# Attention heads' outputs transposed in 32x32 blocks on VectorE in place of TensorE, in a fused adaLN transformer block on one core

## The chip, the cores and the metric

The kernel runs on one core of one Trainium2 chip. The metric is device microseconds of one execution, taken as the median of several runs. Times inside the program come from one profiled execution of it.

## What is computed

One transformer block with adaptive layer norm, B = 1, S = 2048, D = 448, F = 1792, 16 heads of 28 columns, sliding window of 256, all in float32:

```python
mod = (silu(c) @ w_mod).reshape(1, 6, 1, D)       # sa, ca, ga, sb, cb, gb
h = layernorm(x) * (1 + ca) + sa
q, k, v = heads(h @ wqkv)                          # 16 heads of 28
p = softmax(where(0 <= i - j < 256, q k^T * 28 ** -0.5, -1e9))
x = x + ga * (merge_heads(p @ v) @ wo)
h = layernorm(x) * (1 + cb) + sb
x = x + gb * (mish(h @ w1 + b1) @ w2)
```

Every float32 product is made of several float32r passes: each operand is split into a high part (rounded to float32r) and a low part (the rest), and high*high, high*low and low*high are added.

## The kernel before

The rows are worked on in NG = 4 groups of 512 (`GT`). One group of attention is 16 heads, one head is 3 units (`BLOCKS`: six key blocks of 128 by the query blocks that see them), so there are 192 units, and one pass of the main loop (L930 to L981) issues one unit in a software pipeline. Names used below: g is the group, v the unit within it (0 to 47).

In pass u of that loop TensorE is given, in this order: `PV(u - 3, Pl)` (probabilities' low part times v, into the PSUM bank `pv`), `B(u)` (scores transposed, into `sB`, two banks, with mask and row maximum added by extra rows and a bf16 matmul), `A(a, t)` (scores of a head three ahead, into `sA`, two banks, read by VectorE for the row maximum), matmuls of a filler, and `PV(u - 2, Ph)`. ScalarE makes the two exponentials of the unit (`P`, `Ph`, L624 and L625), POOL (GpSimd) their difference `Pl` (L632). The filler (`fill_main`, L844) is a generator of the dense matmuls that belong to other places of the program: the qkv projection of this and the next group, `gen_oT` and `gen_wo` of the group before, `gen_hT` of the next. A second generator (`fill_side`, L863) has layer norm statistics, weights' loads and splits. A credit decides how much filler a unit gets: each pass adds `RATE[g]` (0.48, 0.91, 0.91, 0.65), each step of the filler takes off what it says it costs, and a step that gives no cost takes off `RATE[g]`. Every engine works through its instructions in the order written here; all DMAs stand in SP's queue.

What the change touches is the way from a head's result to the matmul with `wo`:

- `EV` (L646): ScalarE copies a head's result (60 rows: 28 of the high pass, the sum of the probabilities, 3 of zeros, 28 of the low pass; 512 columns) from the one `pv` bank into half of an SBUF tile `O2`. Two heads fill one tile.
- `E`, `E2`, `E3` (L649, L656, L660), once for two heads: four 128x124 transposes on TensorE into the PSUM bank `tr`, a ScalarE copy of the low part (L658), a VectorE reciprocal (L666) and addition (L667), and a POOL multiplication (L669) into `on`, which has rows on partitions and the 448 columns of all heads behind each other. At a group's last pair POOL also doubles the last 64 columns (L671).
- `gen_oT` (L506): when a group is complete, 16 transposes on TensorE (through `tr_chunk`, L232), four to a bank, turn `on` round; ScalarE makes the high part (L516), VectorE the low part (L511), reading the PSUM bank.
- `gen_wo` (L528): 11 passes of 448 columns to each of 4 row tiles, then the residual.
- `M2` (L586), once for two heads: a transpose of the row maxima into bank `tr`, split by VectorE into `mr`, sent by SP's queue into two rows of the `q` tiles. `B` of these heads waits for it.
- `gen_mod_wo` (L468): loads `wo` by rows of 128, scales it by ga on POOL, splits it (ScalarE high, POOL low).

## Time and profile before

| what | us |
|---|---|
| median of 3 runs (731.04 to 731.16) | 731.08 |
| span of the profiled execution, first to last instruction | 727.2 |
| the runs' median above that span | 3.9 |
| TensorE busy | 690.9 (95%) |
| ScalarE busy | 392.3 (54%) |
| VectorE busy | 381.4 (52%) |
| POOL busy | 331.2 (46%) |

In the profile PE is TensorE's matmuls, PEld its weight loads, DVE VectorE, ACT ScalarE and POOL GpSimd. A matmul's row has its own duration, longer than the step to the next matmul, because matmuls overlap; so a share of busy time says little of TensorE's slack, and prices on TensorE are read from the starts of neighbouring rows. Rows on ScalarE overlap by about a tenth of a microsecond in the same way. In the list of waits, "A <- B" is idle time of A that B's instruction ended. In a table by stage, each engine's busy time stands with its count of instructions. Attention runs from 56.4 us to about 422 us: group 0 to 133, group 1 to 235, group 2 to 337, group 3 to 422. Groups 1 and 2 go through the same steps 102 us apart.

### The profile page before, as it was taken

The numbers are of one execution on the slowest core, as the hardware profiler recorded it, in microseconds if no ns is written. First come the engines' busy times: TensorE is split into PE (matmuls) and PEld (weight loads), VectorE is DVE, ScalarE is ACT, GpSimd is POOL, SyncE is SP. The second block draws the span as 40 slices with busy tenths as digits, with TensorE's granted clock in tenths as the row PEclk, the third lists the DMA queues.
The fourth block names the chain that finished last, engine by engine and source line by source line (L and its number), as shares of the span: only waits on it lengthen the run. The fifth ranks groups of instructions, "written<-read, shape, count | busy, mean of one in ns | idle before, by whom it ended". The sixth has DMA issues, their size and how long they took to land.

```text
span 727.2 us, 11903 instructions
## 1 busy us (share of the span) xinstructions
PE 690.9 (95%) x3969; PEld 588.4 (81%) x3969; DVE 381.4 (52%) x1011; ACT 392.3 (54%) x740; POOL 331.2 (46%) x362
## 2 busy tenths in 40 slices
PE   3989989999999999999999899999999999999996
PEld 2767768888889888888887688888888888888885
DVE  4768645687765688655668942334333223322112
ACT  3516777676776667766878984344223222322221
POOL 4725697676666586766778955322010000000002
PEclk9898999999999999999999999999999999999999
DMA  8776564174483354471666175300300020001001
GB/s 201 213 239 190 186 200 135 56 234 130 123 260 132 115 173 147 137 217 56 182 202 191 48 239 166 115 13 1 102 0 1 1 101 1 1 1 51 1 0 51
DMA packets 48121, 83.86 MB, mean 115 GB/s; under 512 B 6126, under 2 KB 26108, under 8 KB 48060
## 3 DMA queue, kind: packets, MB, share of 16 engines
q1 hardware_dynamic: 48060, 83.10, 37.6%
q8 instruction: 32, 0.52, 0.3%
q14 instruction: 29, 0.24, 0.1%
HBM read 53.45 MB, written 29.36 MB: 114 GB/s over the span
## 4 chain that ended last, share of the span: by engine, by line
PE 69%; issue 11%; DVE 8%; ACT 5%; DMA 4%; POOL 2%; SPq 1%; POOLq 0%; DVEq 0%; ACTq 0%
PE z L820 15%; PE pv L642 8%; PE qk L294 7%; PE qk_v L294 5%; PE acc L1000 5%; PE acc L1001 5%; PE acc L999 5%; PE sA L580 4%; PE wo L294 4%; PE sB L610 4%; PE sB L621 3%; DVE junk L582 3%; ACT P L624 2%; PE et L653 1%; DMA wm<-in_w_mod_dram 1%
## 5 line engine op out<-in xcount | busy, mean ns | idle before, releaser
L632 POOL TENSOR_TENSOR Pl<-P,Ph 128x512 fp32r<-128x512 f32 (+2 forms) x192 | 232.9, 1221 | 80.9 <-ACT Ph L625 47.8
L582 DVE CUSTOM_DVE_ANT_0 junk<-sA,mask 128x384 f32<-128x384 f32 (+2 forms) x256 | 135.3, 529 | 100.7 <-PE sA L580 95.4
L828 DVE TENSOR_TENSOR al<-t,ah 128x512 fp32r<-128x512 f32 x56 | 38.8, 692 | 200.9 <-ACT ah L827 200.9
L624 ACT ACTIVATE P<-sB 128x512 f32<-128x512 f32 (+2 forms) x192 | 109.7, 571 | 63.0 <-PE sB L621 56.2
L826 ACT ACTIVATE t<-z,b1c 128x512 f32<-128x512 f32 x56 | 38.5, 688 | 188.6 <-PE z L820 177.7
L625 ACT ACTIVATE Ph<-sB 128x512 fp32r<-128x512 f32 (+2 forms) x192 | 109.3, 569 | 0.0
L580 PE MATMUL sA<-k,q 84*128 84x384 f32 (+2 forms) x256 | 101.0, 399 | 5.7 <-DVE mx L582 5.2
L820 PE MATMUL z<-hhf,w 128*128 128x512 f32 x224 | 89.5, 400 | 0.0
L820 PE MATMUL z<-hlf,w 128*128 128x512 f32 x224 | 88.8, 396 | 0.0
L999 PE MATMUL acc<-w2h,ah 128*128 128x448 f32 x224 | 82.1, 367 | 0.0
L1000 PE MATMUL acc<-w2l,ah 128*128 128x448 f32 x224 | 82.1, 367 | 0.0
L1001 PE MATMUL acc<-w2h,al 128*128 128x448 f32 x224 | 82.0, 366 | 0.0
L642 PE MATMUL pv<-Pl,v 128*60 128x256 f32 (+2 forms) x352 | 74.2, 285 | 5.1 <-POOL Pl L632 5.0
L642 PE MATMUL pv<-Ph,v 128*60 128x256 f32 (+2 forms) x352 | 76.9, 292 | 2.2 <-ACT o L647 2.0
L610 PE MATMUL sB<-q,k 86*128 86x256 f32 (+1 forms) x352 | 75.1, 287 | 0.4 <-DMA q<-mr 0.2
L820 PE MATMUL z<-hhf,w1l 128*128 128x512 f32 x168 | 66.3, 395 | 0.0
L610 PEld LDWEIGHTS sB<-q,k 86*128 86x128 f32 x352 | 62.2, 191 | 2.3 <-DMA q<-mr 0.6
L621 PE MATMUL sB<-fdmask,identr 128*128 128x128 bf16 (+1 forms) x320 | 60.5, 255 | 0.0
L580 PEld LDWEIGHTS sA<-k,q 84*128 84x128 f32 x256 | 49.3, 194 | 12.9 <-DVE mx L582 11.1
L642 PEld LDWEIGHTS pv<-Ph,v 128*60 128x60 f32 x352 | 45.5, 133 | 16.4 <-ACT o L647 4.3
L642 PEld LDWEIGHTS pv<-Pl,v 128*60 128x60 f32 x352 | 44.9, 132 | 16.2 <-POOL Pl L632 9.6
L1008 POOL TENSOR_TENSOR yo<-yo,x 128x448 f32<-128x448 f32 (+1 forms) x4 | 4.2, 1060 | 108.6 <-DVE yo L1005 108.6
(150 smaller groups left out, 1290.6 us busy)
## 6 DMA issues: line engine op xcount, KB each, us to landing
scr<-st SPq DMA_DIRECT2D x24, 512.0 KB
k<-scr SPq DMA_DIRECT2D x48, 252.0 KB
q<-scr SPq DMA_DIRECT2D x64, 168.0 KB
scr<-st SPq DMA_DIRECT2D x32, 256.0 KB
x<-x1d SPq DMA_DIRECT2D x10, 448.0 KB
xin<-in_A_x_dram SPq DMA_DIRECT2D x8, 448.0 KB
xr<-in_A_x_dram SPq DMA_DIRECT2D x16, 224.0 KB
x1d<-xr SPq DMA_DIRECT2D x16, 224.0 KB
```

The lines of the kernel that those rows point to most:

```text
L294: PE.matmul(p, b, a, start=(n == 0), stop=(n == 10))
L580: PE.matmul(p[:, c0:384], q[0:84, t * 128:(t + 1) * 128], k[0:84, t * 128 + c0:t * 128 + 384], start=True, stop=True)
L582: DVE.tensor_tensor_reduce(out=junk[:, c0:384], in0=p[:, c0:384], in1=mask[:, c0:384], scale=1.0, scalar=-3.0e38, op0=ALU.add, op1=ALU.max ...
L610: PE.matmul(p[:, c:c + 128 * (t1 - t0)], k[:, jj * 128:(jj + 1) * 128], q[:, t0 * 128:t1 * 128], start=(n == 0), stop=False, skip_group_ch ...
L624: ACT.activation(P[:, c0:], p[:, c0:], AF.Exp, scale=SCALE)
L625: ACT.activation(Ph[u][:, c0:], p[:, c0:], AF.Exp, scale=SCALE)
L632: eng.tensor_tensor(Pl[u][:, a:b], Pt[u][:, a:b], Ph[u][:, a:b].bitcast(F32), op=ALU.subtract)
L642: PE.matmul(pv[0:60, t0 * 128:t1 * 128], V[j % NV][:, h, :], P[u][:, c:c + 128 * (t1 - t0)], start=(P is Ph and b == 0 and n == 0), stop=F ...
L820: PE.matmul(zb[n], ps[m][1], ps[m][0], start=(m == 0), stop=(m == 10))
L999: PE.matmul(p, ah[n][:, ts], w2h[f], start=(f == 0), stop=False)
L1000: PE.matmul(p, ah[n][:, ts], w2l[f], start=False, stop=False)
L1001: PE.matmul(p, al[n][:, ts], w2h[f], start=False, stop=(f == NF - 1))
```

## The change

The four transposes per pair and the sixteen per group leave TensorE. `wo` is laid out anew so that each head has 32 rows (28 of `wo` and 4 of zeros). With that, a 32x32 block of four heads' results, stacked by 32 partitions, is in the right place for the matmul when every block is transposed by itself, which VectorE has an instruction for. It goes there and back: `EV` stacks four heads (high part and sum in `H4`, low part in `L4`), `N1` adds the two on POOL, `N2` turns the blocks (VectorE) and takes the reciprocal of the sums, `N3` multiplies on POOL, `N4` turns the blocks back into `on`, which is now already transposed. The four steps stand in passes u = 15, 16, 17 and 18, and every 12 passes after. `gen_oT` has no TensorE work left, and its VectorE subtraction reads two SBUF tiles. The bank `tr` is gone; `pv` has two banks, and `M2` takes its bank from `sA`. The padded `wo` is made in device memory by two DMAs early in the program. `wo` has a fourth low part, so `gen_wo` has 12 passes where it had 11.

```diff
+    wod = dram.tile([H, 32, D], F32, name="wod")
...
-    first = [(m, bank(tag, b, f"qk0_{m}"), qk_passes(0, m)) for m, tag, b in ((0, "pv", 1), (3, "tr", 1), (4, "sA", 2))]
+    first = [(m, bank(tag, b, f"qk0_{m}"), qk_passes(0, m)) for m, tag, b in ((0, "pv", 2), (3, "pv", 2), (4, "sA", 2))]
...
-    O2 = []
-    for i in range(2):
-        t = att.tile([128, GT], F32, name=f"o2_{i}")
-        POOL.memset(t[32:64, :], 0.0)
-        O2.append(t)
+    H4 = [att.tile([128, GT], F32, name=f"h4_{i}") for i in range(2)]
+    L4 = att.tile([128, GT], F32, name="l4")
+    POOL.memset(L4, 0.0)
...
-            split_lo(w, wo3[ci], wol[min(ci, 2)], ci, POOL)
+            POOL.tensor_tensor(wol[ci], w, wo3[ci].bitcast(F32), op=ALU.subtract)
...
-        def oT_out(p, ci):
-            DVE.tensor_tensor(ol[:, ci], p, oh[:, ci].bitcast(F32), op=ALU.subtract)
+        def oT_out(ci):
+            DVE.tensor_tensor(ol[:, ci], o[:, ci], oh[:, ci].bitcast(F32), op=ALU.subtract)
         for ci in range(4):
-            p = bank(tag, bufs, f"ot{g}{ci}")
-            tr_chunk([o[:, t] for t in range(4)], ci, p)
-            ACT.activation(oh[:, ci], p, AF.Copy)
-            pipe.add(1, lambda p=p, ci=ci: oT_out(p, ci))
+            ACT.activation(oh[:, ci], o[:, ci], AF.Copy)
+            pipe.add(1, lambda ci=ci: oT_out(ci))
...
-            for ci in range(3):
+            for ci in range(4):
                 ps += [(oh[:, ci, ts], wo3[ci]), (oh[:, ci, ts], wol[ci]), (ol[:, ci, ts], wo3[ci])]
-            ps += [(oh[:, 3, ts], wo3[3]), (ol[:, 3, ts], wo3[3])]
...
     def M2(pr):
-        p = bank("tr", 1, f"mt{pr}")
+        p = bank("sA", 2, f"mt{pr}")
...
-            pvb[i] = bank("pv", 1, f"pv{i}")
+            pvb[i] = bank("pv", 2, f"pv{i}")
...
     def EV(i):
-        r = 64 * (i % 2)
-        ACT.activation(O2[i // 2 % 2][r:r + 60], pvb[i][0:60, :], AF.Copy)
+        r, b = 32 * (i % 4), i // 4 % 2
+        ACT.activation(H4[b][r:r + 32], pvb[i][0:32, :], AF.Copy)
+        ACT.activation(L4[r:r + DH], pvb[i][32:60, :], AF.Copy)
...
+    def N1(qd):
+        POOL.tensor_tensor(H4[qd % 2], H4[qd % 2], L4, op=ALU.add)
+
+    def N2(qd):
+        oq[qd] = att.tile([128, 16, 32], F32, name=f"oq{qd}", tag="oq")
+        DVE.transpose(oq[qd].rearrange("p b j -> p (b j)"), H4[qd % 2])
+        rc4[qd] = att.tile([128, 16, 1], F32, name=f"rc{qd}", tag="rc")
+        DVE.reciprocal(rc4[qd], oq[qd][:, :, DH:DH + 1])
+
+    def N3(qd):
+        o = oq[qd][:, :, 0:DH]
+        POOL.tensor_tensor(o, o, rc4[qd].to_broadcast([128, 16, DH]), op=ALU.mult)
+
+    def N4(qd):
...
+        DVE.transpose(on[g][:, ci], oq[qd].rearrange("p b j -> p (b j)"))
...
+    later.append(lambda: dma(wod[:, 0:DH].rearrange("h r n -> h (r n)"), wo.rearrange("(h r) n -> h (r n)", r=DH)))
+    later.append(lambda: dma(wod[:, DH:32], L4[0:H, 0:D].unsqueeze(1).to_broadcast([H, 4, D])))
...
+        for w, f in ((15, N1), (16, N2), (17, N3), (18, N4)):
+            if u >= w and (u - w) % 12 == 0 and (u - w) // 12 < NS // 4:
+                f((u - w) // 12)
```

Beside that, E, E2 and E3 go, staging tiles shrink from 512 to 448 columns, and the buffers that hold `wo` (later w2) grow from 7 to 8.

How the order of instructions moves is seen at three places, all in the first units of group 1, where the results of group 0 are turned round. TensorE there, before: `ot` is a bank with four transposes of `on`, `sA` the scores for the row maximum, `pv` the head's result.

```order
L621 MATMUL sB_2001<-fdmask,identr 128x256
L580 MATMUL sA_1_2011<-k_3_359,q_1_351 128x384
L232 MATMUL ot_2021<-ident,on_911 128x128 x4
L580 MATMUL sA_2_2029<-k_3_359,q_1_351 128x384
L642 MATMUL pv_1966<-Ph_1944,v_144 60x128
```

TensorE at the same place, now:

```order
L618 MATMUL sB_1971<-fdmask,identr 128x256
L577 MATMUL sA_1_1981<-k_3_360,q_1_352 128x384
L577 MATMUL sA_2_1987<-k_3_360,q_1_352 128x384
L639 MATMUL pv_1931<-Ph_1913,v_145 60x128
L639 MATMUL pv_1931<-Ph_1913,v_143 60x384
```

The transposes are gone and nothing is put in their place: four units that had them have the attention's own matmuls alone. Between v = 4 and v = 11 the filler gave TensorE 11 dense matmuls before and gives 15 now; the units from 12 to 19 have 36 where they had 37. VectorE there, before (`hlo` is the low part of the turned result, `ot` lies in PSUM, `mx` the row maxima):

```order
L666 RECIPROCAL rc_2014<-et_1952 128x8
L667 TENSOR_TENSOR ol_1988<-ol_1988,et_1952 128x224
L582 ISA junk,mx_1885<-sA_2_2029,mask 128x384
L582 ISA mx_1885 128x1
L511 TENSOR_TENSOR hlo_2020<-ot_2021,hho_2019 128x512
L582 ISA junk,mx_1885<-sA_3_2049,mask 128x384
```

VectorE, now (`oq` and `on` are SBUF tiles):

```order
L579 ISA junk,mx_1848<-sA_0_1948,mask 128x384
L579 ISA mx_1848 128x1
L664 STREAM_TRANSPOSE on_1044<-oq_1890 128x512
L193 BN_STATS sta_1957<-xin_844 128x6
L194 BN_AGGR mva_1826<-sta_1957 128x2
L319 TENSOR_TENSOR st_6_1925<-qk_6_1860,st_6_1925 128x512
L511 TENSOR_TENSOR hlo_1955<-on_1044,hho_1954 128x512
L579 ISA junk,mx_1848<-sA_1_1981,mask 128x384
```

The reciprocal and the addition leave this place, a block transpose comes, and the subtraction no longer follows a TensorE instruction. POOL there, before (`Pl` is one unit's difference of exponentials):

```order
L207 TENSOR_TENSOR rsa_1993<-rsa_1993,mhalf 128x4
L632 TENSOR_TENSOR Pl_2009<-P_1977,Ph_1978 128x512
L669 TENSOR_TENSOR on_911<-ol_1988,rc_2014 128x4x56
L671 COPY on_911<-on_911 128x4x64
L632 TENSOR_TENSOR Pl_2047<-P_2005,Ph_2006 128x512
L632 TENSOR_TENSOR Pl_2073<-P_2043,Ph_2044 128x512
```

POOL, now (`h` is `H4`, `l` is `L4`):

```order
L648 TENSOR_TENSOR h_1_367<-h_1_367,l_368 128x512
L629 TENSOR_TENSOR Pl_1881<-P_1842,Ph_1843 128x512
L629 TENSOR_TENSOR Pl_1916<-P_1877,Ph_1878 128x512
L658 TENSOR_TENSOR oq_1890<-oq_1890,rc_1892 128x16x28
L629 TENSOR_TENSOR Pl_1946<-P_1912,Ph_1913 128x512
L208 TENSOR_TENSOR rsa_1960<-rsa_1960,mhalf 128x4
L629 TENSOR_TENSOR Pl_1979<-P_1942,Ph_1943 128x512
L629 TENSOR_TENSOR Pl_2006<-P_1975,Ph_1976 128x512
```

The multiplication and the doubling that stood among the `Pl` right behind `rsa` are gone from there; the multiplication of four heads stands two units earlier. In SP's queue the two DMAs for the padded `wo` stand behind the loads of the fifth head's q and k, ahead of the first later store of q and k.

64 lines of the change are left out of this document (21 added, 43 removed).

## Prediction

> **What bounds the kernel now.** I read the busy shares first, to see whether any engine is full:
>
> ```profile
> PE 690.9 (95%) x3969; PEld 588.4 (81%) x3969; DVE 381.4 (52%) x1011; ACT 392.3 (54%) x740; POOL 331.2 (46%) x362
> ```
>
> TensorE is, on average; the three others stand at half. But two thirds of the change lie in attention, which has stages of its own, so the next view is the busy time by stretch (length, then PE, PEld, DVE, ACT, POOL, the granted TensorE clock, the DMA engines' share and GB/s). The cuts follow the stages of the filler.
>
> ```profile
> 0.00:56.40 56.40, 40.14 (x170) 31.41 (x170) 36.38 (x85) 19.82 (x33) 25.76 (x63) 0.93 0.74 212
> 56.40:88.00 31.60, 29.98 (x186) 23.95 (x187) 24.82 (x78) 24.41 (x54) 19.99 (x21) 0.91 0.58 184
> 88.00:116.00 28.00, 25.03 (x167) 19.47 (x165) 13.98 (x57) 20.88 (x47) 25.95 (x28) 1.00 0.64 202
> 116.00:144.00 28.00, 27.82 (x182) 23.38 (x181) 17.08 (x61) 20.36 (x45) 19.06 (x20) 1.00 0.28 84
> 144.00:160.00 16.00, 15.21 (x111) 12.73 (x109) 13.16 (x40) 12.80 (x25) 12.47 (x14) 1.00 0.60 188
> 160.00:177.50 17.50, 17.30 (x116) 15.41 (x115) 13.77 (x39) 10.26 (x20) 11.23 (x13) 1.00 0.68 207
> 177.50:192.50 15.00, 14.13 (x107) 12.25 (x107) 13.73 (x39) 12.98 (x24) 11.27 (x11) 1.00 0.26 75
> 192.50:235.10 42.60, 42.60 (x289) 37.51 (x288) 24.39 (x82) 29.55 (x58) 27.28 (x23) 1.00 0.63 187
> 337.10:353.80 16.70, 16.62 (x108) 14.04 (x108) 8.75 (x30) 11.27 (x23) 10.81 (x10) 1.00 0.36 111
> 368.00:390.00 22.00, 22.00 (x157) 19.47 (x156) 14.97 (x49) 15.82 (x33) 16.32 (x15) 1.00 0.65 188
> 390.00:422.00 32.00, 27.85 (x208) 22.20 (x206) 28.65 (x70) 29.55 (x58) 30.60 (x30) 1.00 0.33 97
> 422.00:727.20 305.20, 298.42 (x1409) 257.68 (x1407) 90.68 (x145) 99.69 (x160) 40.54 (x49) 0.99 0.15 48
> ```
>
> TensorE fills the stretch, to 98% or more, in 116 to 144, 160 to 177.5, 192.5 to 235.1, 337 to 354, 368 to 390 and from 422 on; the stretches of group 1 have twins 102 us later in group 2. There a TensorE instruction less is time less. Elsewhere it has room: POOL bounds 88 to 116, and 390 to 422 has ScalarE, VectorE and POOL all near full. What TensorE waits for, in the list of waits (total us, times, longest):
>
> ```profile
> PE sA L580 <- DVE mx L582: 5.2, 13, 0.9
> PE pv L642 <- POOL Pl L632: 5.0, 12, 0.8
> PE pv L642 <- ACT o L647: 2.0, 2, 1.2
> ```
>
> **The change part by part.**
>
> *TensorE's transposes of heads.* What four of them cost is the difference of neighbouring starts (start, own duration, row):
>
> ```profile
> 220.21 0.59 PE L653 MATMUL et<-ident,o 124*128 124x124 f32 x4
> 220.55 0.45 PE L294 MATMUL qk_v<-wql,hh 128*128 128x448 f32 x1
> 220.84 0.36 PE L294 MATMUL qk_v<-wq,hl 128*128 128x448 f32 x1
> 221.05 0.37 PE L294 MATMUL qk_v<-wq,hh 128*128 128x448 f32 x1
> ```
>
> The four take 0.34 us (220.21 to 220.55), and the matmul behind them steps 0.29 where its like steps 0.21, so 0.43 in all. How many fall where TensorE is full, from the `et` rows of the same stretches alone (length, PE busy and count):
>
> ```profile
> 116.00:144.00 28.00, 1.17 (x8) 1.00 0.28 84
> 160.00:177.50 17.50, 0.59 (x4) 1.00 0.68 207
> 192.50:235.10 42.60, 2.35 (x16) 1.00 0.63 187
> 337.10:353.80 16.70, 0.59 (x4) 1.00 0.36 111
> 368.00:390.00 22.00, 1.17 (x8) 1.00 0.65 188
> 422.00:727.20 305.20, 0.59 (x4) 0.99 0.15 48
> ```
>
> With the twins of the second and third row that is 64 of 128, 16 groups of four: 16 x 0.43 = **-6.9 us**. The other 16 groups go from places that have room.
>
> *TensorE's transposes of `on`.* The same reading for a group's bank:
>
> ```profile
> 431.26 0.60 PE L232 MATMUL ot<-ident,on 128*128 128x128 f32 x4
> 431.61 0.48 PE L820 MATMUL z<-hhf,w 128*128 128x512 f32 x1
> 431.93 0.39 PE L820 MATMUL z<-hhf,w1l 128*128 128x512 f32 x1
> ```
>
> 0.35 to the next start, which steps 0.32 where 512 columns at the rate above (448 in 0.21) take 0.24: 0.43 again. Of 16 banks the four of group 3 lie here, behind 422: **-1.7**. The other twelve stand at the starts of groups, where TensorE has room.
>
> *The twelfth pass* of `wo` adds 16 matmuls of 448 columns at 0.21 (220.84 to 221.05). Four are behind 422, and I put three of the other twelve in full stretches, since the order has more dense work at v = 4 to 11 and less at 12 to 19: 7 x 0.21 = **+1.4**. Full stretches together: **-7.2**.
>
> *ScalarE, POOL and VectorE* pay for it. Groups of instructions (busy, mean ns | idle before):
>
> ```profile
> L647 ACT ACTIVATE o<-pv 60x512 f32<-60x512 f32 x64 | 37.8, 590 | 22.5 <-PE pv L642 21.6
> L658 ACT ACTIVATE ol<-et 128x224 f32<-128x224 f32 x32 | 11.7, 364 | 0.0
> L632 POOL TENSOR_TENSOR Pl<-P,Ph 128x512 fp32r<-128x512 f32 x155 | 200.0, 1294 | 72.9 <-ACT Ph L625 40.7 <-POOL Pl L632 9.5 <-PE pv L642 8.3
> L669 POOL TENSOR_TENSOR on<-ol,rc 128x224 f32<-128x224 f32 x32 | 18.9, 592 | 23.1 <-ACT Ph L625 11.0 <-DVE ol L667 10.5 <-PE sA L580 1.0
> ```
>
> ScalarE's rows overlap by 0.1, so a copy of 512 columns is 0.48 and one of 224 is 0.26. Per head one long copy is added and half a short one goes, +0.35; over 64 heads +22 us. POOL gets per four heads `N1` (shape and kind of `Pl`: 1.29) and `N3` (twice the columns of `on`: 1.1) for two `on`: +1.2, over 16 tiles +19. Where this binds:
>
> - 88 to 116: the `on` of three pairs leave and one and a half tiles come: 1.5 x 2.4 - 3 x 0.59 = 1.8 on an engine with 2.0 us of room that was already waited for. **+1.5**.
> - 390 to 422: about six heads' share, POOL +1.8, ScalarE +2.0, on engines with 1.4 and 2.5 us of room, and VectorE has 3.3. **+2.5**.
> - In the full stretches both engines have a quarter to a third of room; nothing, but TensorE's gain shrinks that cover by a fortieth.
>
> *VectorE.* No row of before shows the block transpose. The nearest rows by size are a read of 448 columns in SBUF, and the same engine's SBUF to SBUF operation, which spreads widely (min/median/max):
>
> ```profile
> L192 DVE BATCH_NORM_STATS2 stw<-xr 128x6 f32<-128x448 f32 x16 | 10.0, 628 | 0.5
> L222 DVE TENSOR_SCALAR xin<-xin,mva,rsa x12: 498/854/1499, 50.5 to 268.7; 128x448 f32<-128x448 f32 x12
> L667 DVE TENSOR_TENSOR ol<-ol,et 128x224 f32<-128x224 f32 x32 | 10.7, 335 | 0.0
> L666 DVE RECIPROCAL rc<-et 128x8 f32<-128x8 f32 x32 | 6.5, 203 | 0.0
> ```
>
> So 0.5 to 1.5 us; I take 0.65, by the first row, which holds its time. Then per tile 2 x 0.65 + 0.2 replaces 2 x (0.335 + 0.203): +0.4, 7 us in all, beside TensorE's work nearly everywhere, and TensorE no longer waits in line with it. At 1.5 it would be +34 us; that is the first rival. *A rule against the change:* the Trainium skill, VectorE: DVE Perf Modes, section "Rules for kernel authors", gives a 128x128 transpose to TensorE wherever PSUM will do as its destination, and its section "The three transpose paths" has VectorE at 311 ns for 128x128 in bf16. Four of those are an estimate of 1.24 us a tile of 512 columns; by it VectorE gets 19 us more than by 0.65, of which TensorE would feel perhaps an eighth, and the sum would end near 728. No row of before shows it, and both lie within the range.
>
> *The starts of groups 1 and 2* (144 to 160). POOL's multiplication and doubling left of `Pl`:
>
> ```profile
> 153.81 0.40 POOL L671 COPY on<-on 128x256 f32<-128x256 f32 x1
> 155.50 0.45 PE L642 MATMUL pv<-Pl,v 128*60 128x256 f32 x2 [0.41 <-POOL Pl L632]
> ```
>
> The `Pl` that TensorE waits for stands 0.96 us earlier (0.40 and an `on`); the next link, VectorE's row maximum, is close behind, and its `hlo` keeps its length. **-0.8** each, -1.6. At 177.5 to 192.5 and its twin a transpose group goes where TensorE has 0.9 room: -0.3 each, **-0.6**. At 56 to 88 two groups, 0.86, of which two thirds count: **-0.6**.
>
> *Banks.* The second `pv` bank ends waits for the copy of a result, 2.0 us at most in the list above; **-1.0**, as the copies themselves come later. `M2` now takes one of two `sA` banks. 13 of 256 users of these waited, 5.2 us, 0.02 apiece; 32 more users would add 0.65, and if each waited like those 13 (0.4), 12.8. I take **+0.8**, since the 243 others didn't wait.
>
> *The start.* The padded `wo` copies 0.8 MB in device memory, 1.6 MB read and written. At the 212 GB/s of the first stretch that is 7.6 us if everything behind it in SP's queue waits; the queue's next entries are stores and loads of q and k, whose first use lies several us behind. Between 0 and 7.6 I take **+0.7**: the DMA share is 0.74, so most fits in.
>
> Sum: -7.2 + 1.5 + 2.5 - 1.6 - 0.6 - 0.6 - 1.0 + 0.8 + 0.7 = -5.5. The profiled execution's span is 727.2, the median of the runs 731.08, 3.9 above; that part stays. **731.1 - 5.5 = 725.6 us.** Its own range is 721 to 729.5: the small terms at their favourable ends, or `M2`, the start and a long transpose at +4 together.
>
> **The rivals.**
>
> *Slower: VectorE becomes the late link.* The row of L222 above shows one kind of VectorE instruction at 0.50 and the same one at 1.50; the subtraction that reads PSUM does not stretch:
>
> ```profile
> L511 DVE TENSOR_TENSOR hlo<-ot,hho 128x512 fp32r<-128x512 f32 x16 | 11.0, 686 | 6.6 <-ACT hho L516 6.6
> ```
>
> If what stretches L222 is POOL at work in SBUF (a `Pl` is 1.29 us long), then 32 transposes and the twelve `hlo` within attention, which now read and write SBUF alone, may each take 0.43 longer (its mean of 0.93 less 0.50): 44 x 0.43 = 19 us, with the 7 above 26 us. They stand in line ahead of row maxima. VectorE is tight in 56 to 88, 144 to 160, 177.5 to 192.5, their twins and 390 to 422, some 126 of 366 us of attention, a third: +9, and **735** (732.5 to 738). It decides from 0.3 us apiece (5.5 over 44 instructions, of which the tight third counts in full and the rest in a tenth: 5.5 / 18 = 0.3). For it: the spread, and 5.2 us of waits for the row maximum already. Against: VectorE is half idle, and a single delay of 0.4 is mostly covered by `sA`'s second bank. The Trainium skill, SBUF — State Buffer, section "SBUF: two separate sides", has a lock behind such a spread: one port pair is held for a whole instruction by GpSimd, or by a VectorE operation in a 2-port mode or with two SBUF inputs. By it `hlo` would wait and a block transpose, with one source, need not, which halves this rival; the trace agrees so far as L222 and L511 go. Chance 0.27.
>
> *The full gain.* All TensorE work that goes counts: 48 x 0.43 - 16 x 0.21 = 17.3, and with the `pv` waits, less M2 and the start, **713**. Against it: POOL at 25.95 of 28.00 and 30.60 of 32.00 can't give way. Chance 0.10.
>
> *No change.* ScalarE's 22 us and POOL's 19 us more bind wherever TensorE gave room, so that the full stretches turn into ones bounded by the probabilities: **731**, within 1.4. For it: ScalarE's 29.55 and POOL's 27.28 of 42.60 hide a rhythm in which TensorE waits for each unit in turn. Chance 0.13. That the second bank of `pv` does nothing would cost the forecast 1 us only.
>
> **How the numbers follow.** The forecast has 0.50. Faster by more than 0.2% (1.5 us, about what a measurement of this kernel can tell from no change) are the forecast and the full gain: 0.60. Same 0.13, slower 0.27. For 8 in 10 the range leaves out the far end of the full gain and the far end of the slower case: 715 to 737.
>
> **What would show it.** Right: 192.5 to 235 and its twin get shorter by 1.5 us or more each, the end from the last unit to the last instruction by 1.5, and 88 to 116 and 390 to 422 get longer, with POOL near full. The block transpose has a mean of 0.6 to 0.8. Wrong: transposes or `hlo` of over 1 us, and row maxima as the first releaser of TensorE, with more than 10 us (first rival); a start of attention later than 58 us (the DMAs); waits of `M2`'s transposes or of `sA` above 8 us (the bank); or 88 to 116 no longer than before (full gain).

## The result, and the profile after

Median 736.14 us (733.82 to 737.49, 7 runs) against 731.08 (728.18 to 732.45, 7 runs): the ratio is 1.0069, interval 1.0046 to 1.0092. The change makes the kernel slower by 0.7%; forecast were 725.6 us and faster. The busy shares:

```profile
PE 684.7 (93%) x3793; PEld 578.0 (79%) x3793; DVE 398.8 (54%) x995; ACT 422.3 (58%) x772; POOL 351.5 (48%) x357
```

TensorE lost 176 instructions and 6 us of busy time, ScalarE got 30 us, POOL 20 and VectorE 17. To find the place, I cut the span of the changed kernel at its own units: the start, group 0, then for each group its units 0 to 3, 4 to 15 and the rest (group 3: 16 to 27 and 28 to 46), and what lies behind the start of the last unit. Columns as before.

```profile
0.00:58.27 58.27, 40.28 (x170) 31.79 (x171) 36.82 (x85) 20.52 (x34) 25.21 (x62) 0.94 0.79 228
58.27:134.84 76.57, 71.49 (x441) 55.59 (x441) 50.25 (x171) 64.26 (x139) 61.58 (x61) 0.96 0.54 164
134.84:145.64 10.80, 10.62 (x63) 8.67 (x63) 5.83 (x20) 7.94 (x16) 5.61 (x6) 1.00 0.24 77
145.64:172.58 26.94, 24.47 (x147) 20.78 (x146) 23.23 (x60) 19.97 (x37) 21.17 (x20) 0.87 0.62 188
172.58:236.29 63.71, 62.40 (x427) 54.73 (x426) 45.70 (x133) 51.81 (x96) 46.85 (x39) 1.00 0.56 167
236.29:247.25 10.96, 10.80 (x64) 8.84 (x64) 5.88 (x19) 7.88 (x15) 5.76 (x6) 1.00 0.14 41
247.25:274.57 27.32, 24.68 (x148) 20.59 (x146) 22.92 (x60) 19.97 (x37) 21.18 (x20) 0.88 0.59 185
274.57:338.29 63.72, 62.41 (x427) 54.75 (x426) 45.70 (x133) 51.81 (x96) 46.83 (x39) 1.00 0.51 152
338.29:347.19 8.90, 8.90 (x57) 7.53 (x57) 4.61 (x16) 7.06 (x14) 4.62 (x5) 1.00 0.17 52
347.19:371.44 24.25, 21.16 (x134) 17.32 (x133) 16.80 (x45) 20.56 (x39) 20.66 (x17) 0.93 0.63 199
371.44:393.04 21.60, 21.60 (x152) 19.07 (x150) 15.39 (x48) 17.88 (x34) 15.30 (x13) 1.00 0.68 198
393.04:426.86 33.82, 26.53 (x182) 20.28 (x181) 29.97 (x65) 30.23 (x58) 32.04 (x30) 0.97 0.25 73
426.86:732.97 306.11, 299.36 (x1403) 258.04 (x1402) 95.74 (x147) 102.45 (x164) 44.68 (x49) 0.99 0.16 49
```

The same cuts in the kernel before; shown are the stages that will matter, units 4 to 15 of groups 1 to 3 and the last units of group 3:

```profile
144.10:168.21 24.11, 23.32 (x166) 20.01 (x164) 19.89 (x55) 17.99 (x35) 18.05 (x21) 1.00 0.67 210
...
246.20:270.34 24.14, 23.39 (x165) 20.00 (x164) 19.93 (x55) 17.99 (x35) 18.00 (x21) 1.00 0.68 209
...
346.31:368.04 21.73, 21.45 (x158) 18.77 (x157) 14.06 (x46) 18.21 (x36) 16.25 (x15) 1.00 0.70 218
...
390.10:419.84 29.74, 25.59 (x193) 20.47 (x192) 27.59 (x66) 27.29 (x54) 28.52 (x29) 1.00 0.32 92
```

All stages, us:

| stage | before | after | difference |
|---|---|---|---|
| start, to the first scores | 56.45 | 58.27 | +1.8 |
| group 0 | 76.91 | 76.57 | -0.3 |
| units 0 to 3 of groups 1, 2, 3 | 10.74, 11.08, 9.22 | 10.80, 10.96, 8.90 | -0.4 |
| units 4 to 15 of groups 1, 2, 3 | 24.11, 24.14, 21.73 | 26.94, 27.32, 24.25 | +8.5 |
| units 16 to 47 of groups 1, 2 | 66.91, 66.75 | 63.71, 63.72 | -6.2 |
| units 16 to 27 of group 3 | 22.06 | 21.60 | -0.5 |
| units 28 to 46 of group 3 | 29.74 | 33.82 | +4.1 |
| behind | 307.35 | 306.11 | -1.2 |

The sum is +5.8, the difference of the spans of the two profiled executions (the medians differ by 5.1). So the gain was there and was given back at three places of 24 to 27 us each, and in group 3's last units. In units 4 to 15, where the last group's results are turned round, VectorE, ScalarE and POOL are all at least 73% busy in groups 1 and 2, and the granted clock stands below 1. TensorE's scores wait there for VectorE's row maxima, 2.1, 2.3 and 3.1 us in groups 1, 2 and 3; in the kernel before the list of the same units has no such wait. The whole span has 10.0 us of it (5.2 before):

```profile
PE sA L577 <- DVE mx L579: 10.0, 13, 1.5
```

VectorE's rows there, low part of the turned result (`hlo`), and the two block transposes:

```profile
L511 DVE TENSOR_TENSOR hlo<-on,hho 128x512 fp32r<-128x512 f32 x16 | 20.4, 1278 | 2.8 <-ACT hho L514 2.8
...
L652 DVE STREAM_TRANSPOSE oq<-h 128x512 f32<-128x512 f32 x16 | 11.4, 710 | 5.0 <-POOL h L648 4.8
L664 DVE STREAM_TRANSPOSE on<-oq 128x512 f32<-128x512 f32 x16 | 11.3, 708 | 3.7 <-POOL oq L658 3.7
```

The transposes take 0.71 us, near the 0.65 estimated. The subtraction took 0.686 when it read PSUM and takes 1.278 now, as a mean of values from 0.68 up. How the row maxima get late, from VectorE's rows and POOL's at the start of group 1 (start, duration):

```profile
150.77 0.71 DVE L664 STREAM_TRANSPOSE on<-oq 128x512 f32<-128x512 f32 x1
...
152.12 0.66 DVE L319 TENSOR_TENSOR st<-qk,st 128x512 fp32r<-128x512 f32 x1
152.70 0.68 DVE L511 TENSOR_TENSOR hlo<-on,hho 128x512 fp32r<-128x512 f32 x1
153.30 0.55 DVE L579 CUSTOM_DVE_ANT_0 junk<-sA,mask 128x384 f32<-128x384 f32 x1
153.77 0.08 DVE L579 DVE_READ_ACCUMULATOR2_ANT mx<- 128x1 f32 x1
...
156.60 1.79 DVE L511 TENSOR_TENSOR hlo<-on,hho 128x512 fp32r<-128x512 f32 x1 [0.68 <-ACT hho L514]
158.31 0.55 DVE L579 CUSTOM_DVE_ANT_0 junk<-sA,mask 128x384 f32<-128x384 f32 x1
```

```profile
153.62 7.31 POOL L629 TENSOR_TENSOR Pl<-P,Ph 128x512 fp32r<-128x512 f32 x5
```

POOL works without a gap on five `Pl`, and the subtraction that starts at 156.60 lasts 1.79 us: its own 0.69 and most of a `Pl`. The row maximum behind it (`junk`, `mx`) starts at 158.31 only. TensorE's scores wait for both maxima shown:

```profile
153.91 0.44 PE L577 MATMUL sA<-k,q 84*128 84x384 f32 x1 [1.31 <-DVE mx L579]
...
158.92 0.69 PE L577 MATMUL sA<-k,q 84*128 84x384 f32 x1 [0.75 <-DVE mx L579]
```

So there are two things. The first and longer wait stands behind a subtraction of 0.68 us, which nothing held up: between two row maxima VectorE has a block transpose, statistics, `st` and the subtraction in line, as the order ahead of the prediction showed. Only the second wait stands behind a stretched one. The four subtractions of this group take 0.68, 0.96, 1.79 and 1.76 us.

What happens to TensorE's clock meanwhile (the third column from the right):

```profile
152.00:154.00 2.00, 0.69 (x7) 0.42 (x5) 1.83 (x6) 1.98 (x5) 1.62 (x3) 1.00 1.00 351
154.00:156.00 2.00, 1.63 (x10) 1.24 (x11) 1.92 (x5) 1.96 (x5) 2.00 (x2) 0.84 1.04 267
156.00:158.00 2.00, 2.00 (x10) 1.60 (x9) 1.40 (x1) 2.00 (x5) 2.00 (x3) 0.50 0.85 226
158.00:160.00 2.00, 1.25 (x4) 1.04 (x4) 1.97 (x7) 1.15 (x3) 2.00 (x2) 0.50 0.13 43
160.00:162.00 2.00, 2.00 (x8) 1.66 (x8) 1.96 (x3) 0.00 (x0) 1.58 (x2) 0.50 0.10 15
```

Two microseconds in which TensorE is busy for 0.69, then, from 155.3 on, about 7 us at half speed. The second group has the same, group 3 half as much. Busy time of TensorE there is therefore no sign of more work.

### The profile page after: what moved, and what is told of

It reads as the page before. It is cut to its first block, busy times and chain, and to the rows that moved or that the text cites. A ratio compares the mean times of both kernels' runs of the same rounds, so it can differ in the third digit from the quotient of the medians.

```text
span 733.0 us, 11603 instructions
## 1 busy us (share of the span) xinstructions
PE 684.7 (93%) x3793; PEld 578.0 (79%) x3793; DVE 398.8 (54%) x995; ACT 422.3 (58%) x772; POOL 351.5 (48%) x357
## 4 chain that ended last, share of the span: by engine, by line
PE 70%; issue 12%; DVE 7%; ACT 4%; DMA 4%; POOL 3%; SPq 0%; POOLq 0%; DVEq 0%; ACTq 0%
PE z L814 15%; PE pv L639 9%; PE qk L296 7%; PE wo L296 6%; PE sA L577 5%; PE acc L993 5%; PE acc L994 5%; PE acc L992 5%; PE sB L607 4%; PE qk_v L296 4%; PE sB L618 3%; DVE junk L579 2%; DMA wm<-in_w_mod_dram 1%; PE qk L403 1%; ACT P L621 1%
## 5 line engine op out<-in xcount | busy, mean ns | idle before, releaser
L629 POOL TENSOR_TENSOR Pl<-P,Ph 128x512 fp32r<-128x512 f32 (+2 forms) x192 | 236.3, 1244 | 90.2 <-ACT Ph L622 46.3
L639 PE MATMUL pv<-Pl,v 128*60 128x256 f32 (+2 forms) x352 | 76.9, 293 | 10.3 <-POOL Pl L629 8.5
L607 PE MATMUL sB<-q,k 86*128 86x256 f32 (+1 forms) x352 | 77.2, 294 | 2.4 <-DMA q<-mr 1.8
L607 PEld LDWEIGHTS sB<-q,k 86*128 86x128 f32 x352 | 63.8, 197 | 4.8 <-issue 2.3
L639 PEld LDWEIGHTS pv<-Ph,v 128*60 128x60 f32 x352 | 47.6, 136 | 14.0 <-issue 1.2
```

Source lines behind the costliest of these rows:

```text
L607: PE.matmul(p[:, c:c + 128 * (t1 - t0)], k[:, jj * 128:(jj + 1) * 128], q[:, t0 * 128:t1 * 128], start=(n == 0), stop=False, skip_group_ch ...
L629: eng.tensor_tensor(Pl[u][:, a:b], Pt[u][:, a:b], Ph[u][:, a:b].bitcast(F32), op=ALU.subtract)
L639: PE.matmul(pv[0:60, t0 * 128:t1 * 128], V[j % NV][:, h, :], P[u][:, c:c + 128 * (t1 - t0)], start=(P is Ph and b == 0 and n == 0), stop=F ...
```

## The experiments

Three theories: (1) TensorE stands idle for want of other work, its clock falls, and that is the cost; (2) VectorE's subtraction, held up by POOL, is the late link; (3) the bank that the row maxima's transpose now shares. Since up to 134 us most of the kernels below run the same instructions and yet group 1 starts at 134 to 141 us in their profiles, I judge each by its stage as well as by its median. The stage is units 4 to 15 of a group (26.94, 27.32 and 24.25 us in the changed kernel); a table at the end of this section has it for all runs. Medians of different runs are compared through their ratios to the kernel before, which was measured again beside each (changed kernel: 1.0069).

**Dense work in the gap.**

```diff
+            p = bank("mm" if g < NG - 1 else "tr", 2, f"ot{g}{ci}")
+            for n in range(4):
+                PE.matmul(p[:, 0:D], wo3[n][:, 0:128], wo3[n], start=(n == 0), stop=(n == 3))
             ACT.activation(oh[:, ci], o[:, ci], AF.Copy)
```

> The changed kernel with four dense matmuls of 448 columns (result unused) added to each of the 16 steps that turn a group's result round, where TensorE had its transposes before. Theory 1 (clock): TensorE stands idle there, so its granted clock falls to 0.50 for 3.4 or 6.8 us in four places, about 10 us of half speed in sum; with dense work there the clock stays above 0.95 in 144 to 168 and its twin, and the time falls to 731 to 733 though TensorE does 13 us more work. Theory 2 (VectorE's subtraction, stretched by POOL from 0.69 to 1.28 us, is what holds TensorE, the clock is a by-product): the added work comes on top, 737 to 741, and VectorE stays the releaser. Theory 3 (the bank of M2): no less waiting for sA, 736 to 740.

740.77 us, ratio to before 1.0136 (1.0114 to 1.0159). The stage in group 1:

```profile
150.92:177.47 26.55, 24.83 (x164) 21.66 (x162) 23.68 (x60) 19.97 (x37) 21.25 (x20) 1.00 0.62 191
```

The clock holds at 1.00, and the stage takes 26.55 us in groups 1 and 2 and 22.72 in group 3: 0.4, 0.8 and 1.5 less than in the changed kernel, not the 2.5 to 3.2 that were lost. That is 2.7 of the 8.5 us, and not all of it can be the clock's: a run below without the padded copy (`direct_wo`) has the changed kernel's own instructions in this stage, and takes 26.51 us in group 1 with the clock at 1.00 and nothing added, and in group 3 22.70 us, as short as here, with the clock at 0.92. The median is higher through the start and group 0, which the edit doesn't touch and which differ between profiles, and through 3.2 us behind attention, where the added work of group 3 stands.

**TensorE's old transposes, unused.**

```diff
+            p = bank("mm" if g < NG - 1 else "tr", 2, f"ot{g}{ci}")
+            tr_chunk([o[:, t] for t in range(4)], ci, p)
             ACT.activation(oh[:, ci], o[:, ci], AF.Copy)
```

> The changed kernel with the old 16 transposes of four 128x128 blocks a group put back on TensorE, result unused (0.43 us each step, 7 us of TensorE work in all). Theory 1 (clock): TensorE is busy a little more in the places where the clock falls; if transposes count as activity the clock holds at some of them and the time is 732 to 735; if not, the clock falls as before and the time is 736 to 738. Theory 2 (VectorE): 736 to 738, the four of group 3 behind attention cost 1.7.

745.41 us, ratio 1.0211 (1.0187 to 1.0235), far beyond every forecast. The stage in group 1, and a wait of group 3's transposes behind attention:

```profile
148.97:175.76 26.79, 23.41 (x164) 20.45 (x162) 23.23 (x60) 19.97 (x37) 20.88 (x20) 1.00 0.60 189
```

```profile
PE ot L233 <- DVE on L666: 4.5, 1, 4.5
```

The loss is in that last place: the part behind attention is 315.8 us long, 9.7 more, since these transposes stand in TensorE's line ahead of the feed-forward matmuls and wait for VectorE's last block transpose; the wait shown is 4.5 of the 9.7. In attention the clock holds at 1.00 through the stage, and it still takes 26.8: the clock again isn't the bound. This run is the base for the one below that gives the subtraction an operand in PSUM.

**No subtraction.** `oT_out` is left out, and the low passes read the high part:

```diff
-            pipe.add(1, lambda ci=ci: oT_out(ci))
...
-                ps += [(oh[:, ci, ts], wo3[ci]), (oh[:, ci, ts], wol[ci]), (ol[:, ci, ts], wo3[ci])]
+                ps += [(oh[:, ci, ts], wo3[ci]), (oh[:, ci, ts], wol[ci]), (oh[:, ci, ts], wo3[ci])]
```

> The changed kernel without the 16 VectorE subtractions for the low part of the turned result; the matmuls that read it read the high part again, so the low part's product is wrong by that much. VectorE loses 20 us, 15 of them at the starts of groups 1 to 3. Theory 2 (the stretched subtraction): TensorE's longest wait for the row maximum (1.31 us at the start of group 1) goes, the time falls by 5 to 8, to 728 to 731, and the clock stays at 1. Theory 1 (idle TensorE since its filler has nothing to give): the units there are bounded by the probabilities and VectorE anyway, TensorE idles on, the clock still falls in one or two of the places, 732 to 735. Theory 3 (bank): under 2 us less, 734 to 736.

729.56 us, ratio 0.9990 (0.9970 to 1.0010): 0.8% less than the changed kernel, level with the kernel before. The stage in groups 1 and 3:

```profile
148.60:173.41 24.81, 23.09 (x147) 19.91 (x146) 18.54 (x56) 19.97 (x37) 20.07 (x20) 0.93 0.65 204
```

```profile
346.92:367.64 20.72, 19.54 (x134) 16.12 (x133) 12.43 (x41) 19.46 (x38) 16.89 (x14) 1.00 0.72 213
```

24.8 and 20.7 where the changed kernel has 26.9 and 24.3; group 2 gains less, 26.2 for 27.3. The time is as theory 2 forecast, but the clock still falls in groups 1 and 2, which theory 2 had not expected. And the run takes away the whole subtraction, which the kernel before has too and fits into 24.1 us.

**The banks as before** (`pv` one bank, the maxima's transpose one of its own):

```diff
...
-        p = bank("sA", 2, f"mt{pr}")
+        p = bank("mt", 1, f"mt{pr}")
...
-            pvb[i] = bank("pv", 2, f"pv{i}")
+            pvb[i] = bank("pv", 1, f"pv{i}")
```

> The changed kernel with the banks as they were before: one for the heads' results and one of its own for the transposed row maxima. Theory 3 (bank): waits of the row-maximum scores for VectorE fall from 10.0 to about 5 us, the time by 3 to 5, to 731 to 733, and the clock falls in fewer places. Theories 1 and 2: no change in the places where the clock falls, 735 to 738 with the waits for the copy of a result back (2 us).

740.78 us, ratio 1.0166 (1.0122 to 1.0209). Waits of the whole span:

```profile
PE pv L639 <- ACT l L645: 12.3, 23, 1.6
...
PE sA L577 <- DVE mx L579: 9.1, 12, 1.6
```

The scores wait for VectorE nearly as much as in the changed kernel (9.1 us for 10.0), and the time grows, so as an account of the whole loss theory 3 falls. What comes back is the wait for the copy of a result: 12.3 us where the kernel before had 2.0. The copy has become two, and the second `pv` bank hides that; the two bank edits together are worth 4.0 us by the profiled spans (737.0 for 733.0), not 0.2. By stage it is less simple: with the old banks group 0 takes 3.0 us more and units 16 to 47 of groups 1 and 2 take 2.0 more each, but units 4 to 15 take 1.4, 1.8 and 1.3 less. Theory 3 is therefore not ruled out for the stage itself.

**The subtraction with one operand in PSUM**, by way of TensorE's transposes, for the results of groups 0 to 2 (the blocks are turned once more, so the output differs):

```diff
+            s = o[:, ci]
+            if g < NG - 1:
+                s = bank("mm", 2, f"ot{g}{ci}")
+                tr_chunk([o[:, t] for t in range(4)], ci, s)
-            ACT.activation(oh[:, ci], o[:, ci], AF.Copy)
-            pipe.add(1, lambda ci=ci: oT_out(ci))
+            ACT.activation(oh[:, ci], s, AF.Copy)
+            pipe.add(1, lambda ci=ci, s=s: oT_out(ci, s))
```

> The changed kernel with the 16 TensorE transposes a group put back for groups 0 to 2, into a bank that ScalarE's high part and VectorE's low part now read in place of the SBUF tile (the blocks are turned a second time, so the result differs). VectorE's subtraction then reads one operand in PSUM. If two SBUF operands are what lets POOL hold it up, its mean falls from 1.28 to about 0.69 us in these groups (12 of 16), and against the run with transposes but the SBUF operand (units 4 to 11 of group 1 in 18.2 us, 18.2 in group 2) those units take 16 to 17 us; the time is 730 to 733. If the length of the subtraction is not what counts, but TensorE's lack of other work, those units stay at 18 us and the time at 735 to 738. The run with transposes had lost 9.7 us behind attention by group 3's; here these are left out, and the end behind the last unit is back at 306 us.

732.45 us, ratio 1.0029 (1.0015 to 1.0043). The subtraction's two forms, and the stage in group 1:

```profile
L511 DVE TENSOR_TENSOR hlo<-ot,hho 128x512 fp32r<-128x512 f32 x12 | 8.2, 686 | 5.0 <-ACT hho L518 5.0
...
L511 DVE TENSOR_TENSOR hlo<-on,hho 128x512 fp32r<-128x512 f32 x4 | 5.2, 1328 | 0.5 <-ACT hho L518 0.5
```

```profile
148.19:173.66 25.47, 23.48 (x163) 20.41 (x162) 20.82 (x60) 19.97 (x37) 19.77 (x20) 1.00 0.63 199
```

In one kernel, 0.686 us with an operand in PSUM (the results of groups 0 to 2) and 1.328 with both in SBUF (those of group 3, behind attention). At the same place, the stage of group 1, the run with the same transposes and the operand in SBUF has 0.68, 0.98, 1.35 and 1.78 us, and this run 0.68 to 0.69 four times. At the same clock of 1.00 the stage is shorter than in that run by 1.3, 1.1 and 1.0 us in groups 1, 2 and 3, and TensorE's waits for row maxima in the whole span fall from 10.7 to 4.8 us: the hold-up costs about 3.4 us. Theory 2 is shown, but it isn't the whole 8.5.

**ScalarE's second copy and POOL's addition left out**, singly and together. The low pass of the heads' results is then missing from the output.

```diff
-        ACT.activation(L4[r:r + DH], pvb[i][32:60, :], AF.Copy)
```

> The changed kernel without ScalarE's second copy of each head's result (64 copies of 28 rows, 0.5 us each; the low pass of the probabilities is left out of the result). Tells the cost of ScalarE's added work, 31 us. If ScalarE bounds the tail of group 3 (units 28 to 47, 33.8 us against 29.7 before) and the POOL-bound stretch hardly gains, the tail falls by 3 to 4 us and the time to 731 to 733; if POOL bounds it, the tail falls by under 1 us and the time is 734 to 736. The clock falls at the starts of groups as before.

```diff
-        POOL.tensor_tensor(H4[qd % 2], H4[qd % 2], L4, op=ALU.add)
+        pass
```

> The changed kernel without POOL's addition of the two halves (16 of 1.29 us, the low pass left out of the result). If POOL bounds the tail of group 3 and the units 20 to 35 of group 0 (units 28 to 31 took 8.60 us there, 6.56 before), these two places give back 2 and 1 to 2 us and the time is 732 to 733.5; if ScalarE bounds the tail, only the 1 to 2 us of group 0 come back, 734 to 735.5.

> The changed kernel without the second copy on ScalarE and without the addition on POOL (the low pass left out of the result). Each alone left the last 20 units of group 3 at 33.8 and 35.6 us (33.8 with both, 29.7 in the kernel before). If these units are bounded by ScalarE and POOL in turn, taking both away brings them to 30 to 32 us and the time to 726 to 729; if something else bounds them (VectorE, or a clock that falls), they stay above 33 and the time is 729 to 731.

729.79 us (ratio 0.9999, 0.9984 to 1.0015) without the copy, 738.29 (1.0112, 1.0079 to 1.0145) without the addition, 727.91 (0.9965, 0.9947 to 0.9983) without both. First the stage in group 1 without the copy, then the last units of group 3 without the addition, then these without both:

```profile
146.41:171.68 25.27, 22.20 (x148) 18.62 (x146) 22.65 (x60) 17.71 (x33) 21.05 (x22) 1.00 0.64 200
```

```profile
395.62:431.24 35.62, 28.05 (x182) 21.79 (x181) 32.10 (x65) 30.78 (x58) 28.79 (x28) 0.90 0.23 69
```

```profile
385.89:418.88 32.99, 26.06 (x183) 20.89 (x181) 31.00 (x65) 26.55 (x51) 28.69 (x27) 0.95 0.25 73
```

My expectation put the copy's price in the tail of group 3; it lies in the stage, 1.7, 2.0 and 2.6 us, and without both the stage is the same within 0.1 us. The tail stays at 33.9 without the copy, and 33.0 without both. In the kernel before POOL was 96% busy there (28.52 of 29.74); in the changed kernel it is 95% (32.04 of 33.82), with 3.5 us more busy time. But without both POOL is back at 28.69 and ScalarE below its old 27.29, and the tail still takes 3.3 us more than before; VectorE then stands at 94% (31.00 of 32.99). That VectorE holds the tail is only argued, since no run takes its work away there. Why POOL's addition left out makes the whole slower (738.3) I can't settle: of the 5.4 us that its profile is longer than the changed kernel's, 3.5 are at the start, ahead of the first instruction left out, and the clock is at 0.90 in the tail and 0.82 in group 2's stage.

**Useful dense work in the gap**: six of the output projection's matmuls that need the high part alone, two in each turning step but the first (the other two of the eight stand behind the last step, in `gen_wo`).

```diff
+            if g < NG - 1 and ci:
+                wo_mms(g, ci - 1)
...
+    def wo_mms(g, ci):
+        oh, ol = OT[g]
+        for n, b in enumerate((wo3, wol)):
+            PE.matmul(WO0[g][:, 0:D], oh[:, ci, 0:128], b[ci], start=(ci + n == 0), stop=False)
+        for cj in range(4 if ci == 3 else 0):
+            PE.matmul(WO0[g][:, 0:D], ol[:, cj, 0:128], wo3[cj], start=False, stop=(cj == 3))
...
```

> The changed kernel with the first eight dense matmuls of the output projection's first row tile (those that need the high part alone) issued between the four steps that turn a group's result round, two a step, and its low passes at the end. TensorE gets 0.4 us of useful work in each of the units where it stood idle, with no work added. Theory 1 (idle TensorE lets the clock fall): the clock falls in fewer of the four places, the time is 732 to 734. Theory 2 (VectorE's stretched subtraction is the bound): 735 to 737, the same waits for the row maximum.

735.68 us, ratio 1.0103 (1.0053 to 1.0154), no measurable change. The stage in group 1:

```profile
148.47:174.96 26.49, 23.16 (x152) 19.32 (x150) 23.37 (x60) 19.98 (x37) 20.35 (x19) 1.00 0.67 208
```

The clock stays at 1.00 in groups 1 to 3, and the stage takes 26.49, as long as with dense filling though no work is added: theory 2's forecast.

**The DMA for the padded `wo`**, and the kernel before again:

```diff
     def gen_mod_wo():
+        later.append(lambda: dma(wod[:, 0:DH].rearrange("h r n -> h (r n)"), wo.rearrange("(h r) n -> h (r n)", r=DH)))
...
-    later.append(lambda: dma(wod[:, 0:DH].rearrange("h r n -> h (r n)"), wo.rearrange("(h r) n -> h (r n)", r=DH)))
```

> The changed kernel with the large one of the two added DMAs (784 KB of wo into its padded place in device memory) issued not ahead of attention but in front of the loads that read it, behind the group's layer norm. If it is what keeps the row maxima's small DMA from landing (TensorE's first scores waited 1.80 us for it, none before), attention starts at 55.5 to 57.5 us instead of 58.3 (58.3 to 61.8 in the other runs that have it) and the time falls by 1.5 to 3.5, to 732.5 to 734.5. If the later start is chance, attention starts at 58 to 61 and the time stays at 735.5 to 737.

> The kernel before, profiled a second time, to see how much the start of attention and each group differ between two profiles of one program. Theory that the added DMAs delay the start: attention starts at 56.0 to 57.5 again. Theory that the start is chance: it lies anywhere from 56 to 62. Each group within 0.5 us of the first profile (76.9, 101.8, 102.0, 82.7).

738.04 us (1.0105, 1.0084 to 1.0126) and, one run, 728.89. The kernel before starts attention at 56.43 us in the second profile (56.45 in the first), group 0 takes 77.08, and the three stages repeat within 0.04 us. The changed kernel's first scores:

```profile
58.27 0.41 PE L607 MATMUL sB<-q,k 86*128 86x384 f32 x1 [1.80 <-DMA q<-mr]
```

They wait 1.80 us for the 4 KB transfer of the row maxima, which has 784 KB ahead of it. With the big transfer later, attention starts at 57.10 and the first scores wait 0.3, but the wait returns some units on (2.3 us of the 2.6):

```profile
PE sB L608 <- DMA q<-mr: 2.6, 2, 2.3
```

and group 0 takes 80.6 us, 4.0 more, of which this wait explains 2.3. Over all runs the link is plain: in the twelve profiles that issue the big transfer ahead of attention the first scores wait 1.7 to 4.0 us for row maxima, in the four that don't 0.3 to 0.6.

**The subtraction on POOL** (`DVE.tensor_tensor` to `POOL.tensor_tensor` in `oT_out`):

> The changed kernel with the subtraction for the low part moved from VectorE to POOL (16 of 1.29 us, both operands in SBUF). There is then no VectorE instruction there that POOL could hold up. If POOL has room at the starts of groups (74 to 87% busy in those units), the waits for row maxima go as they did without the subtraction, units 4 to 11 of group 1 take 16 to 17.5 us (18.4 now) and the time is 730 to 733; if POOL becomes the bound there, TensorE waits for the probabilities' low part instead and the time is 735 to 739.

743.61 us, ratio 1.0189 (1.0159 to 1.0219). The stage in group 1:

```profile
152.00:179.55 27.55, 24.55 (x147) 20.77 (x146) 19.84 (x56) 20.10 (x37) 24.91 (x24) 0.88 0.59 184
```

VectorE is down to 19.84 us, POOL up to 24.91 of 27.55, so POOL becomes the bound, as one half of the expectation had it; the time is above the 735 to 739 given for that.

**An operand in PSUM without TensorE, no padded copy, and both.** In the first, ScalarE copies the turned tile to a bank:

```diff
+            s = o[:, ci]
+            if g < NG - 1:
+                s = bank("mm", 2, f"ot{g}{ci}")
+                ACT.activation(s, o[:, ci], AF.Copy)
-            ACT.activation(oh[:, ci], o[:, ci], AF.Copy)
+            ACT.activation(oh[:, ci], s, AF.Copy)
```

> The changed kernel with one more ScalarE copy a step for groups 0 to 2: the turned tile goes to a PSUM bank, and the high part and VectorE's low part read it there. No TensorE work is added, ScalarE gets 12 copies (0.5 to 0.6 us each). If two SBUF operands are what lets POOL hold the subtraction up, its mean falls to 0.69 us for these 12, units 4 to 11 of group 1 take 16 to 17.2 us (18.4 now), and the time falls by 3 to 6, to 730 to 733. If not, the subtraction stays above 1.1 us, and ScalarE's copies make it 736 to 739.

In the second each head's rows go straight to their place:

```diff
-            later.append(lambda ci=ci, t=t: dma(t, wod[4 * ci:4 * ci + 4].rearrange("h r n -> (h r) n")))
+            POOL.memset(t, 0.0)
+            for h in range(4):
+                later.append(lambda h=h, r=(4 * ci + h) * DH, t=t: dma(t[32 * h:32 * h + DH], wo[r:r + DH, :]))
...
```

> The changed kernel without the padded copy of wo in device memory: each head's 28 rows are loaded straight to their place in a tile that POOL set to zero (16 loads of 49 KB in place of 4 of 224 KB, a 784 KB and a 112 KB DMA). If the big DMA's bytes ahead of the attention's loads cost 2 to 4 us, attention starts at 55.5 to 57.5 us, group 0 takes 76 to 78 us, and the time is 732 to 734. If the start differs for another reason, the time stays at 735 to 738.

> Both changes together. If the two costs are separate and are what was missed, they add up: 5 to 9 us less, 727 to 731, the same as the kernel before or up to 0.4% faster. If they are one (a later start only shifts the rest), the time is that of the better of the two alone.

> Without the padded copy, and with eight dense matmuls of the output projection between the four turning steps, VectorE's subtraction as in the changed kernel (two SBUF operands). The clock holds in groups 1 to 3 but VectorE stays the bound there: 731.5 to 734, no better than without the padded copy alone by more than 1 us. If the clock were the cost, 727 to 730.

739.11 us (1.0124, 1.0099 to 1.0149), 736.16 (1.0099, 1.0066 to 1.0132), both 738.23 (1.0123, 1.0102 to 1.0144), and the second with the dense work in the gap 736.75 (1.0112, 1.0083 to 1.0141). If the theories behind them held, all four were to be faster than the changed kernel, and none is. For the operand in PSUM, the subtraction's wait in the whole span, and the stage in group 2:

```profile
DVE hlo L511 <- ACT hho L518: 9.9, 9, 2.3
```

```profile
252.82:279.50 26.68, 23.45 (x148) 19.91 (x146) 21.02 (x60) 22.16 (x41) 19.77 (x20) 0.94 0.60 189
```

The subtraction takes 0.69 us, as forecast; but now it waits 9.9 us for ScalarE (2.8 in the changed kernel), which has 22.16 of 26.68 us to do. The late link has moved by one engine, and the stage in group 1 is even longer (28.87). Without the padded copy the first scores wait 0.6 us only; attention still starts at 57.0 to 58.7, and a wait of 1.1 us for `M2`'s share of the `sA` banks, which the kernel before doesn't have, stands ahead of it there as in the changed kernel. And the sixteen small loads stand in SP's queue, twelve of them in a row, ahead of a pair of row maxima:

```profile
89.60 7.34 SPq L59 DMA_DIRECT2D wop<-in_A_wo_dram  x12
97.04 1.39 SPq L59 DMA_DIRECT2D q<-mr  x2
```

TensorE waits 2.3 us for that pair, and group 0 takes 79.2. With dense work in the gap as well, the clock was to hold in groups 1 to 3; in group 1 it fell (0.88, stage 29.42). No version that computes everything beats the kernel before.

**The stage in all runs**, us (granted clock):

| run | group 1 | group 2 | group 3 |
|---|---|---|---|
| kernel before | 24.11 (1.00) | 24.14 (1.00) | 21.73 (1.00) |
| changed kernel | 26.94 (0.87) | 27.32 (0.88) | 24.25 (0.93) |
| big DMA later | 27.13 (0.87) | 27.38 (0.88) | 24.24 (0.93) |
| no padded copy | 26.51 (1.00) | 25.51 (0.93) | 22.70 (0.92) |
| dense work, unused | 26.55 (1.00) | 26.55 (1.00) | 22.72 (1.00) |
| transposes, unused | 26.79 (1.00) | 26.77 (1.00) | 22.69 (1.00) |
| useful dense work | 26.49 (1.00) | 26.49 (1.00) | 23.23 (1.00) |
| the same, no padded copy | 29.42 (0.88) | 26.54 (1.00) | 23.24 (1.00) |
| no subtraction | 24.81 (0.93) | 26.21 (0.87) | 20.72 (1.00) |
| operand in PSUM by TensorE | 25.47 (1.00) | 25.70 (1.00) | 21.67 (1.00) |
| operand in PSUM by ScalarE | 28.87 (0.82) | 26.68 (0.94) | 24.63 (0.93) |
| the same, no padded copy | 26.66 (0.94) | 26.68 (0.94) | 26.60 (0.87) |
| subtraction on POOL | 27.55 (0.88) | 27.67 (0.88) | 24.71 (0.86) |
| old banks | 25.50 (0.93) | 25.49 (0.93) | 22.97 (0.93) |
| no second copy | 25.27 (1.00) | 25.32 (0.93) | 21.64 (1.00) |
| no addition | 26.52 (1.00) | 28.15 (0.82) | 22.70 (0.92) |
| neither | 25.37 (0.93) | 25.28 (0.93) | 21.65 (1.00) |

The second to fourth rows have the same instructions in this stage, and still differ by up to 1.9 us: what was done before the stage changes how the engines' instructions meet in it. A single difference of that size in this table is therefore no proof of a cause. What holds beyond that is what agrees over the groups, or between runs: the operand in PSUM by TensorE against the unused transposes, and the second copy left out, with the addition and without it.

## Why the prediction was wrong

- **The starts of groups: this is the step that failed.** It said that `hlo` "keeps its length" and gave -0.8 for each of two starts, nothing for the third, and it gave ScalarE's second copy no price there at all. Measured: +2.8, +3.2 and +2.5, together +8.5 where -1.6 stood. The forecast followed `Pl`, which comes earlier; but VectorE's row maximum, "close behind" by the prediction, became the late link, with 7.5 us of TensorE's waits in the three stages and none listed there before. The order had shown that a block transpose would stand in line ahead of a row maximum and that `hlo` would read two SBUF tiles, and the rival's paragraph had the row that speaks of it; I had weighed it for the rival only, not for my own sum. Of the parts the runs show two: the hold-up of the subtraction, about 3.4 us, and ScalarE's second copy, 1.7 to 2.6 us a start when it goes. They overlap and needn't add up. The clock's share is open: the fall costs 0.4 us in group 1, by the run with the same instructions at 1.00, and two executions of the changed kernel had the same span, 733.0, at mean clocks of 0.974 and 0.991. The banks' share is open too.
- **The slower rival was right in its mechanism and, by luck, in its time** (735). It let 32 transposes and twelve `hlo` stretch; the transposes hold 0.70 to 0.71 us each. It gave the subtraction 0.43 us more; it was 0.59. And VectorE holds TensorE up at the starts, not in a third of attention. What carried the time from 725.6 to 736.1, ScalarE's copy, the start and the tail among it, is not what made up its +9. The sign that it named did come: `hlo` over 1 us.
- **The full stretches gave more than forecast.** Units 16 to 47 of groups 1 and 2, 16 to 27 of group 3 and the end gave 7.9 us. The -7.8 forecast with 177.5 to 192.5 also has 116 to 144 and 337 to 354 in it; without these it is 6.5. And of the 3.2 us that units 16 to 47 gained in each group, 2.0 hang on the banks, by the run that undoes them. (7 x 0.21, the twelfth pass, is 1.5 and not 1.4.)
- **The tail was mis-sized**: +2.5 forecast, +4.1 measured. POOL has 3.5 us more busy time there, I had counted 1.8: `N1` and `N3` less the `on` that go are 1.9 of it, about what I had counted; the rest is in the `Pl`, which take some 2 us more. TensorE's wait for them went from 0.7 to 4.0 us:

```profile
PE pv L639 <- POOL Pl L629: 4.0, 5, 1.3
```

  Yet with POOL's busy time back at 28.69 the tail kept 3.3 of its 4.1, so what bounds it is open.
- **The start was mis-sized**: +0.7 forecast, +1.8 measured. The DMA share of 0.74 said little; what counts is one small transfer behind a large one. Without the large one attention still starts at up to 58.7 us, so there is another cause, perhaps `M2`'s bank.
- **The banks were mis-sized together**: -0.2 forecast for the two edits, -4.0 by the profile of the run that undoes them, because the copy of a result is two copies now. Group 0 came out at -0.3; the forecast's terms for it, +1.5, -0.6 and two groups of transposes between 116 and 133, make 0.0.
- **The transposes' length** was nearly right (0.65 estimated, 0.71 measured), and the estimate of 1.24 us from the figure for bf16 in the Trainium skill, VectorE: DVE Perf Modes, section "The three transpose paths", was too long.

Of the rules: the Trainium skill, SBUF — State Buffer, section "SBUF: two separate sides", has a lock that a VectorE operation with two SBUF inputs and a GpSimd operation take in turn. The runs agree: 1.328 us with two SBUF operands, 0.686 with one in PSUM, and 0.71 without spread for transposes of one SBUF source. POOL pays as well: its busy time in the stage of group 1 falls from 20.88 to 19.77 us when the subtraction reads PSUM. The rule on the clock in the Trainium skill, TensorE: Matmul & The Clock Gate, section "Why this matters for your kernels", speaks of gaps of more than 3 us. Here the clock fell to 0.50 though no single idle time of TensorE's matmuls at that place was over 1.31 us (2 us of it were busy for 0.69); the measurement decides. In the run without the padded copy the clock stayed at 1.00 through two such stretches, of 0.71 and 0.55 us busy in 2, so what makes it fall is not settled by these runs.

## What to carry to other kernels

Work taken from the engine that is full on average must not be given to the one that is late in the stage where it lands: look at the stage's own table, and at the line behind the moved instruction. An operand that moves from PSUM to SBUF changes a VectorE instruction's length even if its shape stays, when POOL is at work beside it. And moving a cause to another engine gave nothing here, since three engines stood within a quarter or so of full: the subtraction on POOL made POOL the bound (743.6 us), the operand copied by ScalarE made VectorE wait for ScalarE (739.1).
